# An attention and feed-forward block on one core: layer-norm statistics of odd tiles on ScalarE, key/value groups re-timed on VectorE and GpSimd, division issued in another place, two weight loads moved

## The chip, the cores and the metric

The kernel runs on one core of a Trainium2 chip. The metric is device time in microseconds (us). A core has a matmul engine (TensorE, "PE" in the profile; its weight loads are shown as "PEld"), a vector engine (VectorE, "DVE"), an activation engine (ScalarE, "ACT"), a general engine (GpSimd, "POOL") and an engine that here only issues DMAs (SyncE, "SP"). Each has its own queue of instructions and they wait for each other through semaphores. SBUF is the large on-chip memory; PSUM is the small one, where matmuls accumulate; the program uses it in banks of 512 fp32 columns.

The mean TensorE clock granted in the profiled executions was 0.999 or 1.0. Ratios are compared between calls, microseconds only within one.

## The reference

```python
x = A_x                                                     # 1 x 2048 x 1024, bf16
# attention:
qkv = layernorm(x) @ wqkv                                   # 32 heads of 32
phi = lambda t: jnp.where(t > 0, t + 1, jnp.exp(t)) + 1e-6
pq, pk = phi(q), phi(k)
kv  = einsum("bhsd,bhse->bhde", pk, v);   z = sum over s of pk
o   = einsum(pq, kv) / (einsum(pq, z) + 1e-6)
h   = x + o @ wo
# feed-forward, F = 3584:
hn  = layernorm(h)
g   = hn @ W_gate
h2  = h + ((g * (g > 0)) * (hn @ W_up)) @ W_down
```

It is linear attention: no row of scores is ever formed. `kv` and `z` are summed over all 2048 tokens first; then each query tile is multiplied with them ("num", which carries the denominator in extra columns), divided, transposed and multiplied with `wo`.

## The kernel before

The program runs in stages: start-up, the first token tiles with plain products, then alternating key groups and value groups for pairs of token tiles (k2 to k7, v3 to v7), eight query groups (q00 to q03, then q10 to q13), an output stage (division, transposes, `wo`, second layer norm), and the feed-forward part, which takes about two thirds of the time.

Keys, values, queries and the feed-forward products use a Strassen-Winograd scheme: a 2 x 2 block product is made of seven block products in place of eight. The price is sums of blocks beforehand (VectorE and GpSimd subtract weights from weights, VectorE adds token blocks) and copies of partial sums from bank to bank (ScalarE). One group:

```python
prod(a, X(0, 0), W(0, 0), True, "P1")
ident_act(bank(b), bank(a), ..., name + "fk1")      # ACT: copy P1 into bank b
hook(1)
prod(f, SX(2), TW(2), True, "P7")
ident_act(s7, bank(f), ..., name + "s7")            # ACT: copy P7 to SBUF
hook(2)
prod(b, SX(1), TW(1), False, "P6")                  # needs fk1
ident_act(bank(c), bank(b), ..., name + "fk2")      # ACT
hook(3)
prod(a, X(1, 0), W(1, 0), False, "P2");  e11(a)     # first of four outputs
hook(4)
prod(c, SX(0), TW(0), False, "P5")                  # needs fk2
ident_act(sc, bank(c), ..., name + "sc")            # ACT
s22 = e22(bank(f), ..., sc); s22[0]()
hook(5)
prod(b, X(1, 1), TW(3), False, "P4")
s21 = e21(bank(b), ..., s7); s21[0]()
hook(6)
prod(c, SX(3), W(1, 1), False, "P3")
pend[1] = list(e12(bank(c), B_bank[c]))             # rest of the outputs: done in
pend[2] = list(s22[1:])                             # hooks 1, 2, 3 of the NEXT group
pend[3] = list(s21[1:])
```

`hook(i)` first runs what the previous group left in `pend[i]`, then the side work of this group. All engines take their instructions in the order in which this code issues them, so a hook decides behind what a side job stands in its engine's queue. The outputs of key and query groups go through `phi`: an exponential on ScalarE, then on VectorE a clamp of it (`min 1, + 1e-6`) and `max(t + 1, clamped)`. In value groups the outputs are an add on VectorE ("value add").

The side work in the key/value groups:

```python
def ln1_stats(st):                       # two bn_stats, one bn_aggr, one add on DVE, pow on Pool
    ln1_k[st] = ln_stats(x1[:, i, :], ...)
    run(pool_q, {5: 8, 6: 5, ...}.get(st, 7) if st >= 5 else 0)   # Pool: weight subtractions

def h_k3(p=p):  kvacc(2p-2); kvacc(2p-1); ln1_stats(2 * p + 4)
def h_v1(p=p):  x_sums(p + 1)                                   # four token-block sums, DVE
def h_v2(p=p):  ln1_norm(2 * p + 4); T1d(2 * p + 4)             # normalise, DMA transpose
def h_v5(p=p):  ln1_stats(2 * p + 5)
def h_v7(p=p):  ln1_norm(2 * p + 5); T1d(2 * p + 5)
k_group(p, {3: h_k3});   v_group(p, {1: h_v2, 3: h_v1, 5: h_v5, 7: h_v7})
```

Here `run(pool_q, n)` issues `n` subtractions to GpSimd with no condition but that their inputs are there.

Query groups and output stage:

```python
def a2(st):                              # num matmuls, then add, reciprocal, multiply on DVE
    ...                                  # ("division"), then the DMA transpose T3d of the result
for r in range(2):
    for ct in range(NG // 2):
        if r == 1: hooks[6] = lambda t=ct: a2(t)
        q_group(r, ct, hooks)
flush()
for t in range(NE, NST + LAG + 1):
    a4(t - LAG)                          # wo matmuls, h = ... + x on DVE, LN2 statistics on ACT
    a4_norm(t - LAG - 1)
    a2(t)
    if t in (5, 7, 9, 11, 18, 19):
        load_w_next()                    # 512 KB weight load, same DMA queue as the transposes
    ...
for q in range(NWR):
    load_wraw(q)                         # raw down-weights: first needed in the feed-forward part
```

## Time and profile before

The time was 759.61 us, the median of three runs (759.15 to 759.61). The page's first part gives each engine's busy time; its fourth part gives what the chain of work that ended last consists of.

```profile
PE 737.7 (97%) x3547; PEld 337.2 (45%) x3603; DVE 545.6 (72%) x1083; ACT 291.2 (38%) x500; POOL 82.3 (11%) x148
...
PE 84%; DVE 8%; ACT 2%; issue 2%; SPq 1%; DMA 1%; POOL 0%; DVEq 0%; ACTq 0%; POOLq 0%
```

TensorE bounds the kernel, but "97% busy" does not say how near the end that is. The Trainium skill, Perfetto Trace Analysis, section "Identifying the Most-Contended Engine", warns that matmul busy time is a poor measure of it, because matmuls are pipelined. The trace agrees: a 512-column matmul has a mean record of 379 ns but the next one starts 216 ns later, so a record covers up the first 0.16 us of every gap. I therefore use starts only: for each stage, its length less the sum of its matmuls, each at the spacing it has in an undisturbed stretch (0.2158 us for 512 columns, 0.0585 us for the short ones of the accumulation and of num). Some matmuls have no record (3547 records beside 3603 weight loads); where a distance is longer by just one spacing, the missing matmul is counted in. What remains is lost TensorE time. The Trainium skill, TensorE: Matmul & The Clock Gate, section "Wait — 56ns, not 53.3ns?", gives 215.7 ns for the warm spacing, which agrees with 0.2158 us.

| stage, before | from to (us) | lost TensorE time (us) |
|---|---|---|
| start-up | 1.4 to 39.0 | 3.68 |
| keys and values | 39.0 to 126.25 | 8.71 |
| query groups q00 to q03 | 126.25 to 152.7 | 1.32 |
| query groups q10 to q13 | 152.7 to 180.6 | 1.87 |
| output stage | 180.6 to 245.24 | 3.79 |
| feed-forward | 245.24 to the end | 0.08 |
| sum | 756.8 | 19.45 |

The view by windows gives busy time of each engine in a stretch. These are the key/value groups, the query groups and the output stage.

```profile
core 0: us, PE busy (x) PEld busy (x) DVE busy (x) ACT busy (x) POOL busy (x), PEclk, DMA share, GB/s
52.30:126.20 73.90, 67.95 (x355) 29.99 (x360) 60.05 (x117) 37.95 (x70) 32.69 (x49) 1.00 0.18 41
126.20:180.60 54.40, 52.98 (x274) 23.16 (x273) 44.78 (x93) 33.14 (x62) 0.00 (x0) 1.00 0.35 107
180.60:245.20 64.60, 61.28 (x345) 30.48 (x352) 47.94 (x66) 29.19 (x43) 20.10 (x48) 1.00 0.84 199
```

In the first stretch DVE is busy 60.05 of 73.9 us: no engine is full on the average, but DVE is nearest to it after PE. What PE waited for is shown by the view of waits of PE (columns after the colon: us in total, times, longest):

```profile
PE ps L602 <- ACT ps L607: 3.9, 7, 1.2
PE ps L602 <- DMA RE<-RE: 2.3, 3, 1.2
PE ps L602 <- ACT RX L607: 1.9, 2, 0.9
PE ps L602 <- DVE RE L989: 0.6, 1, 0.6
```

L607 are the copies on ACT (fk1, fk2, s7, sc), "RE<-RE" are the DMA transposes after the division, L989 is the division. So PE waits for ACT, but ACT is only half busy. Why does ACT come late? Its own waits in 52 to 126 us name DVE, and most of all the value add at L900, which must empty a bank before fk1 may write it:

```profile
ACT ps L607 <- DVE RE L900: 13.3, 7, 3.4
```

And why is DVE late? The groups of instructions by shape, in the same window (columns: busy us, mean ns of one, idle before):

```profile
L644 DVE TENSOR_SCALAR RX<-RX 128x512 bf16<-128x512 bf16 x20 | 9.0, 451 | 11.2 <-ACT RX L640 11.2
L647 DVE SCALAR_TENSOR_TENSOR RE<-RX 128x512 bf16<-128x512 f32 x5 | 4.3, 858 | 0.2
L647 DVE SCALAR_TENSOR_TENSOR RE<-ps,RX 128x512 bf16<-128x512 f32 x10 | 6.9, 692 | 0.3
```

L644 is the clamp, 0.29 us when alone and 451 ns on the average here. L647 is the max of phi: with both inputs in SBUF it takes 858 ns on the average, with one input in PSUM 692. The timeline of all engines around one late product, the start of group k5 (columns: start us, length us, engine, line, operation, output<-input, count, idle before and releaser):

```profile
77.88 3.30 POOL L739 TENSOR_TENSOR RH<-RO 128x256 f16<-128x256 bf16 x4
...
78.79 1.11 DVE L647 SCALAR_TENSOR_TENSOR RE<-RX 128x512 bf16<-128x512 f32 x1
...
79.82 0.76 DVE L644 TENSOR_SCALAR RX<-RX 128x512 bf16<-128x512 bf16 x1
...
81.64 0.74 DVE L764 TENSOR_TENSOR RWG<-RAB 128x512 f16<-128x512 bf16 x2
...
83.23 0.68 DVE L900 TENSOR_TENSOR RE<-ps,RX 128x512 bf16<-128x512 f32 x1
...
83.94 0.58 ACT L607 ACTIVATE ps<-ps 128x512 f32<-128x512 f32 x1 [3.41 <-DVE RE L900]
...
84.58 1.04 PE L602 MATMUL ps<-RC,RWG 128*128 128x512 f16 x4 [1.23 <-ACT ps L607]
```

Read it backwards. The product P6 starts at 84.58 after PE stood still for 1.23 us; it waited for fk1 (83.94), which waited 3.41 us for the value add (83.23), which stood behind the token-block sums (from 81.64), behind clamp and phi. Beside these Pool runs four subtractions from 77.88 to 81.2, and the clamp takes 0.76 us in place of 0.29, the phi op 1.11 in place of 0.69. The late phi ops cost PE once more just before: the copy sc, at 79.93, waits 1.21 us for one of them, and the last product of the value group 0.94 us for sc.

In the query groups the chain runs over ACT. The timeline of ACT in group q01, from fk1 to fk2:

```profile
134.66 0.58 ACT L607 ACTIVATE ps<-ps 128x512 f32<-128x512 f32 x1 [2.04 <-PE ps L602]
135.15 0.59 ACT L640 ACTIVATE RX<-ps 128x512 bf16<-128x512 f32 x1
135.63 0.60 ACT L607 ACTIVATE RX<-ps 128x512 f32<-128x512 f32 x1
...
136.63 0.61 ACT L607 ACTIVATE ps<-ps 128x512 f32<-128x512 f32 x1
```

Between fk1 and fk2 stand the exponential of the last group's e12 (135.15), s7 (135.63) and another exponential; ACT is idle for 2.04 us before fk1.

Last, DVE at the start of the feed-forward part waits for the first raw down-weight load (the view names no releaser, but the trace has the load landing at 253.03 us); after that it is in time, and PE loses 0.08 us in the whole part:

```profile
253.10 1.55 DVE L588 TENSOR_TENSOR RW<-RW 128x512 f16<-128x512 bf16 x4 [4.04 <-issue]
254.58 0.68 DVE L1171 TENSOR_TENSOR RAB<-ps,RAB 128x512 bf16<-128x512 f32 x1
```

### The profile page before, as it was taken

The page shows a single profiled execution, that of the slowest core. Times are in us where ns is not written, and L with a number is a line of the kernel's source. Part 1 is how long each engine was busy: PE and PEld are TensorE (multiplying, and loading weights), DVE is VectorE, ACT ScalarE, POOL GpSimd, SP SyncE. Part 2 cuts the span into 40 slices and gives each one's busy share as a digit, 9 for nine tenths or more (in the row PEclk, how much of TensorE's full clock was granted, in tenths as well). Part 3 has the DMA queues.
Part 4 walks back from the last instruction along what each step waited for, and adds up shares of the span by engine and source line. Part 5 has one row for each costly group of instructions (what it writes and reads, how often), then busy time and mean ns, then how long its engine had stood idle before and what let it go on. Part 6 is the DMA issues. An engine that isn't in the chain of part 4 may idle for free.

```text
span 756.8 us, 10080 instructions
## 1 busy us (share of the span) xinstructions
PE 737.7 (97%) x3547; PEld 337.2 (45%) x3603; DVE 545.6 (72%) x1083; ACT 291.2 (38%) x500; POOL 82.3 (11%) x148
## 2 busy tenths in 40 slices
PE   8999889999999999999999999999999999999998
PEld 3444334344544444444444444444444444444443
DVE  7978885889766798878877584847768686663343
ACT  4344545665850545454454100025454544520000
POOL 2746730000360000000000000000000000000000
PEclk9999999999999999999999999999999999999999
DMA  9753112402799786665445799743232231026664
GB/s 301 199 84 85 29 28 100 166 15 55 180 238 240 234 274 200 186 174 169 139 139 178 227 289 284 229 143 111 61 108 85 83 111 56 1 77 185 207 191 134
DMA packets 160225, 113.38 MB, mean 150 GB/s; under 512 B 51504, under 2 KB 141360, under 8 KB 160176
## 3 DMA queue, kind: packets, MB, share of 16 engines
q1 hardware_dynamic: 160176, 112.75, 52.3%
q8 instruction: 28, 0.46, 0.2%
q14 instruction: 21, 0.17, 0.1%
HBM read 85.46 MB, written 15.73 MB: 134 GB/s over the span
## 4 chain that ended last, share of the span: by engine, by line
PE 84%; DVE 8%; ACT 2%; issue 2%; SPq 1%; DMA 1%; POOL 0%; DVEq 0%; ACTq 0%; POOLq 0%
PE ps L602 84%; ACT ps L607 1%; DVE RX L644 1%; DVE RAB L647 1%; SPq L512 1%; DVE RE L647 1%; DVE RE L989 1%; DVE RWG L764 1%; ACT RX L640 1%; DVE RE L900 1%; DMA RE<-RE 1%; DVE st L615 1%; DVE RX L839 0%; SPq L508 0%; DVE RXH L629 0%
## 5 line engine op out<-in xcount | busy, mean ns | idle before, releaser
L607 ACT ACTIVATE ps<-ps 128x512 f32<-128x512 f32 x150 | 87.5, 583 | 199.5 <-PE ps L602 170.8
L602 PE MATMUL ps<-RC,RO 128*128 128x512 f16 x672 | 154.2, 379 | 0.0
L602 PE MATMUL ps<-RW,RAB 128*128 128x512 f16 (+1 forms) x681 | 150.1, 379 | 0.6
L602 PEld LDWEIGHTS ps<-RW,RAB 128*128 128x128 bf16 (+1 forms) x692 | 67.7, 98 | 81.6
L602 PE MATMUL ps<-RH,RWG 128*128 128x512 bf16 x435 | 103.0, 379 | 0.7
L602 PEld LDWEIGHTS ps<-RC,RO 128*128 128x128 f16 x672 | 65.7, 98 | 79.3
L607 ACT ACTIVATE RE<-ps 128x512 f32<-128x512 f32 x120 | 71.0, 597 | 76.1 <-PE ps L602 53.9
L602 PE MATMUL ps<-RC,RWG 128*128 128x512 f16 x296 | 71.1, 379 | 2.8 <-ACT ps L607 2.8
L602 PEld LDWEIGHTS ps<-RH,RWG 128*128 128x128 bf16 x448 | 43.8, 98 | 52.9
L1171 DVE TENSOR_TENSOR RAB<-ps,RAB 128x512 bf16<-128x512 f32 x28 | 19.3, 690 | 65.4 <-PE ps L602 65.4
L602 PE MATMUL ps<-RW,RE 128*128 128x512 bf16 x248 | 57.0, 379 | 2.8 <-DMA RE<-RE 2.3
L602 PE MATMUL ps<-RH,RO 128*128 128x512 bf16 (+1 forms) x242 | 58.3, 379 | 0.7
L602 PE MATMUL ps<-RAB 128*128 128x512 bf16 x239 | 56.6, 379 | 1.3 <-ACT RAB L691 0.7
L607 ACT ACTIVATE RAB<-ps 128x512 bf16<-128x512 f32 x56 | 33.4, 597 | 61.6 <-PE ps L602 61.6
L1102 DVE TENSOR_TENSOR RO<-RWG,RO 128x512 f16<-128x512 bf16 x108 | 45.3, 420 | 1.8
L602 PEld LDWEIGHTS ps<-RC,RWG 128*128 128x128 bf16 (+1 forms) x296 | 28.5, 98 | 38.9 <-ACT ps L607 5.4
L623 POOL TENSOR_TENSOR rstd<-ve,neghalf 128x1 f32<-128x1 f32 x24 | 14.4, 601 | 281.2 <-DVE ve L620 281.2
L1178 DVE TENSOR_TENSOR RE<-ps,RE 128x512 f32<-128x512 f32 x56 | 38.4, 690 | 5.0 <-ACT RE L607 5.0
L1102 DVE TENSOR_TENSOR RO<-RWG 128x512 f16<-128x512 bf16 x108 | 40.6, 417 | 0.0
L615 DVE BATCH_NORM_STATS2 st<-RE 128x6 f32<-128x512 bf16 x48 | 30.7, 680 | 12.8 <-DMA RE<-h_scr 11.9
L644 DVE TENSOR_SCALAR RX<-RX 128x512 bf16<-128x512 bf16 x64 | 23.1, 361 | 22.3 <-ACT RX L640 22.3
L1183 DVE TENSOR_TENSOR RE<-ps,RE 128x512 f32<-128x512 f32 x56 | 38.1, 681 | 0.0
(114 smaller groups left out, 792.0 us busy)
## 6 DMA issues: line engine op xcount, KB each, us to landing
RWG<-in_B_W_gate_dram SPq DMA_DIRECT2D x28, 512.0 KB, 3.7
RWG<-in_B_W_up_dram SPq DMA_DIRECT2D x28, 512.0 KB, 4.7
RW<-t_scr SPq DMA_DIRECT2D x56, 256.0 KB, 3.2
RW<-in_B_W_down_dram SPq DMA_DIRECT2D x42, 256.0 KB, 3.8
RW<-in_B_W_down_dram SPq DMA_DIRECT2D x14, 512.0 KB, 4.0
t_scr<-RW SPq DMA_DIRECT2D x14, 512.0 KB, 4.9
RE<-in_A_x_dram SPq DMA_DIRECT2D x23, 256.0 KB, 4.7
RAB<-in_A_wqkv_dram SPq DMA_DIRECT2D x8, 512.0 KB, 8.2
```

The costliest lines, as they stand in the source:

```text
L512: return PL.add("sp", lambda e: e.dma_start_transpose(dst_ap, src_ap), reads=reads, writes=writes, slot=slot, name=name)
L602: lambda e: e.matmul(out_ap, lhsT, rhs, start=start, stop=stop, skip_group_check=skip),
L607: PL.add("act", lambda e: e.activation(out=dst, in_=src, func=func), reads=reads, writes=writes, name=name)
L615: PL.add("dve", lambda e, c=c: e.bn_stats(out=st6[:, k, c * 6:(c + 1) * 6], in_=src_full[:, c * BCH:(c + 1) * BCH]), reads=[src_chunk_bufs ...
L623: PL.add("pool", lambda e: e.tensor_tensor(out=rstd[:, k, :], in0=ve[:, k, :], in1=neghalf[:], op=ALU.pow), reads=[B_ve[k], B_neghalf], wr ...
L640: PL.add("act", lambda e: e.activation(out=Et[:, k, :], in_=src, func=ACTF.Exp), reads=[src_buf], writes=[B_E[k]], name=name + "_exp")
L644: PL.add("dve", lambda e: e.tensor_scalar(out=Et[:, k, :], in0=Et[:, k, :], scalar1=1.0, scalar2=1e-6, op0=ALU.min, op1=ALU.add), reads=[] ...
L647: PL.add("dve", lambda e: e.scalar_tensor_tensor(out=dst_ap, in0=src, scalar=C1, in1=Et[:, k, :], op0=ALU.add, op1=ALU.max), reads=[src_bu ...
L1102: PL.add(eng, lambda e: e.tensor_tensor(out=Tring[:, k, j], in0=in0, in1=in1, op=ALU.subtract), reads=reads, writes=[B_T[k][j]], name="T%d ...
L1171: PL.add("dve", lambda e: e.tensor_tensor(out=hh[:, f1, 0:SBW], in0=bank(BA[1]), in1=r11[:, rr, :], op=ALU.mult), reads=[B_bank[BA[1]], B_ ...
L1178: PL.add("dve", lambda e, w=w: e.tensor_tensor(out=ftmp[:, 4 + w, :], in0=bank(BF_[w]), in1=ftmp[:, 2 + w, :], op=ALU.add), reads=[B_bank[ ...
L1183: PL.add("dve", lambda e, w=w: e.tensor_tensor(out=ftmp[:, 6 + w, :], in0=bank(BB[w]), in1=ftmp[:, w, :], op=ALU.add), reads=[B_bank[BB[w] ...
```

## The change

The intent: take work off DVE where it makes ACT and PE late, keep Pool away from DVE's sensitive ops, and let transposes leave earlier. The diff, cut to its core (renamed buffers and unchanged arithmetic left out):

```diff
+        def act_stats(src, src_bufs, junk, junk_buf, sv, svb, name):
+            def mean():   # ACT: Identity, scale 1/D, accum_out
+            def square(): # ACT: Square, scale D**-0.5, accum_out; then three small ops on Pool
+            return mean, square
+        def pool_piece(n=1):
+            for _ in range(min(n, len(pool_q))):
+                pool_q.pop(0)(PL.prog["act"][-1])   # waits for the ACT op issued last
         def ln1_stats(st):
-            run(pool_q, {5: 8, 6: 5, 7: 4, 8: 5, 9: 5, 10: 5}.get(st, 7) if st >= 5 else 0)
         # w_sums:
-                def go(d):
+                def go(d, dep):
                     PL.add(eng, ... op=ALU.subtract), reads=reads, writes=[btw[j]],
+                           deps=[dep], name=...)
         # sgroup, after P3:
-            pend[1] = list(e12(bank(c), B_bank[c]))
+            s12 = list(e12(bank(c), B_bank[c]))
+            if isq:                       # query groups only
+                s12.pop(0)()              # the exponential of e12, at once
+            pend[1] = s12
         # key/value groups, A, B = 2p + 4, 2p + 5:
+            def h_k1(): pool_piece(2); ln1_stats(A)      # last two p: x_sums instead
             def h_k3(): kvacc(2p-2); kvacc(2p-1)
-                        ln1_stats(2 * p + 4)
-            def h_v1(): x_sums(p + 1)
-            def h_v2(): ln1_norm(2 * p + 4); T1d(2 * p + 4)
-            def h_v5(): ln1_stats(2 * p + 5)
-            def h_v7(): ln1_norm(2 * p + 5); T1d(2 * p + 5)
-            k_group(p, {3: h_k3}); v_group(p, {1: h_v2, 3: h_v1, 5: h_v5, 7: h_v7})
+            def h_k5(): pool_piece(2); m_, q_ = ln1_stats_act(B); m_(); sq.append(q_)
+            def h_k6(): q_(); x_sums(p + 1)
+            def h_v3(): pool_piece(2)                    # last two p only
+            def h_v5(): pool_piece(2)
+            def h_v6(): ln1_norm and T1d of A, then of B
+            k_group(p, {1: h_k1, 3: h_k3, 5: h_k5, 6: h_k6})
+            v_group(p, {3: h_v3, 5: h_v5, 6: h_v6})
         # query groups:
-                    hooks[6] = lambda t=ct: a2(t)
+                    hooks[6] = lambda t=ct: a2_num(t)
                 q_group(r, ct, hooks)
+                if r == 1:
+                    pend[1].insert(1 if ct + 1 < NG // 2 else 0, lambda t=ct: a2_div(t))
         # output stage:
-                a4(t - LAG)
+                a4_mm(t - LAG)
+                a2_num(t); a2_div(t)
+                a4_h(t - LAG)
                 a4_norm(t - LAG - 1)
-                a2(t)
-            if t in (5, 7, 9, 11, 18, 19):
+            if t in (5, 7, 18, 19):
                 load_w_next()
+        load_w_next()
+        load_w_next()
         for q in range(NWR):
             load_wraw(q)
```

So the division of query tile t no longer stands in hook 6 of its own group but in hook 1 of the next, behind the clamp of the phi whose exponential was issued early; and in the output stage it stands in front of h, not behind it.

## The prediction

> **What bounds the kernel.** TensorE: page part 1 gives PE 97% of a 756.8 us span, and part 4 puts 84% of the last chain on matmul. In the timeline the feed-forward part (245 us to the end, about two thirds of the span) starts a 512-column matmul every 0.216 us without a gap; nothing is to be won there. Pricing every matmul at that rate (the 128-column ones at 0.059) leaves 19.4 us of lost PE time, an estimate from those starts, all before 245 us: start-up 3.7, key/value groups (52 to 126 us) 8.8, query groups (126 to 181) 3.2, output stage (181 to 245) 3.8. The change leaves the start-up alone, so 15.7 us (2.1%) is the most it can win.
>
> **Key/value groups.** By windows, DVE is 90% busy in 66 to 98 us, PE 87%. The timeline shows why: beside Pool's subtractions (0.67 us each) the bf16 clamp takes 0.75 us instead of 0.29, the phi op 1.11 instead of 0.69, the normalisation 0.91 instead of 0.54. The Trainium skill, SBUF — State Buffer, "Who interferes with whom", says that such DVE ops contend with GpSimd for a shared port pair; these durations agree. DVE then runs late, ACT's evictions wait for it ("ACT waited for DVE", 11.3 us in 54 to 110 us), and PE waits 1.5 to 1.8 us before each late product. The change takes about 1.7 us of DVE statistics per pair of tiles away, gates Pool's pieces behind chosen ACT ops, and moves the token-block sums out of the crowded place. It adds two ACT passes per odd tile, about 2.3 us (1.06 each plus the accumulator reads, as in the output stage), put where ACT idles 2.04 us before the value group's first eviction; so they delay that one by 0.1 to 0.3 us. I expect this stage to keep 2.5 to 3.3 us of its loss: gain 5.8.
>
> **Query groups.** The exponential issued before the next group's first eviction takes one 0.5 us step from the ACT chain that ends in the second "fk2" copy, where PE waits (0.25 to 0.45 us per group). In the last four DVE is nearly full (7.0 us of work in 7.0), and the first num matmul after them waits 1.0 us for the division behind h. Issuing exponentials early and h after the division gains 0.9 + 2.0.
>
> **Output stage.** PE waits 2.9 us for transposes that land late (a backlog in the DMA queue: the transpose of tile 12 is ready at 219.7, issued at 226.4). Earlier division, and weight loads 2 and 3 out of the way, should remove nearly all: gain 2.8.
>
> **Given back.** Loads 2 and 3 now stand in front of loads 4, 5 and the first raw down-weight load, which already holds DVE for 4.0 us at 249 to 253 us. I expect that load about 3 us later, DVE late in the first feed-forward pair, and PE losing about 1 us there: a new gap where there was none.
>
> **Sum.** 5.8 + 2.9 + 2.8 - 1.0 = 10.5, less 0.7 for surprises: 749.8 us, 8 in 10 between 747.2 and 753.2. Faster by over 2%: 0.03; within 2%: 0.96; slower: 0.01.
>
> **What would show it.** Right: DVE clamp and phi ops mostly at 0.29 and 0.69 us; no PE gap over 1 us before 126 us; no PE wait on the RE transposes; feed-forward starting about 11 us earlier; a DVE wait on the raw weight load longer than 4.0 us. Wrong: value-group evictions waiting for the ACT statistics by over 0.5 us; DVE waiting for the paired xn transposes (2.7 us to land before); Pool still stretching DVE; a stall of 2 us or more in the first two feed-forward pairs.

## The result and the profile after

The changed kernel took 749.0 us (median of four runs, 748.72 to 749.52) beside 759.53 (759.15 to 759.61). The ratio is 0.9863, 95% interval 0.9846 to 0.988. It is computed as the mean time of the fast runs of one kernel over that of the other's of the same rounds, so it is not quite the ratio of the medians. By the measure used here (2%) the two are the same; the predicted 749.8 us is close, and the range 747.2 to 753.2 held. A repeat on another chip gave 749.3 us and 0.987.

Parts 1 and 4 of the page:

```profile
PE 737.0 (99%) x3547; PEld 337.8 (45%) x3603; DVE 537.3 (72%) x1067; ACT 299.9 (40%) x516; POOL 87.5 (12%) x148
...
PE 89%; DVE 4%; ACT 3%; issue 2%; SPq 0%; DMA 0%; DVEq 0%; POOL 0%; ACTq 0%; POOLq 0%
```

The span of the profiled execution went from 756.8 to 747.4 us. PE has the same 3547 matmuls and the same busy time, in a shorter span; DVE's share of the last chain fell from 8 to 4%. The windows of the same three stages, with the same columns as before:

```profile
52.80:120.40 67.60, 66.74 (x355) 30.01 (x360) 51.56 (x105) 44.24 (x82) 31.64 (x48) 1.00 0.22 48
120.40:173.20 52.80, 52.80 (x274) 23.09 (x272) 42.50 (x89) 34.19 (x62) 0.00 (x0) 1.00 0.38 110
173.20:234.60 61.40, 60.64 (x346) 30.63 (x352) 48.24 (x66) 29.18 (x43) 19.55 (x40) 1.00 0.82 193
```

The key/value stretch is 6.3 us shorter for the same 355 matmuls; DVE does 8.5 us less in it and ACT 6.3 us more. The query stretch is 1.6 and the output stage 3.2 us shorter. PE's waits in the whole span are now these; the 1.4 us behind Pool are in the start-up and were there before:

```profile
PE ps L604 <- POOL RXH L475: 1.4, 1, 1.4
...
PE ps L604 <- DVE RE L1219: 0.6, 1, 0.6
PE ps L604 <- DVE RXH L1062: 0.4, 1, 0.4
PE ps L604 <- ACT ps L609: 0.2, 1, 0.2
```

The waits behind ACT's copies fell from 5.8 us (3.9 and 1.9) to 0.2, and those behind the transposes are gone. Two are new: L1219, in the feed-forward part, and L1062, the op that computes h in the output stage. ACT no longer waits for a value add in 52 to 126 us; its longest waits are for PE itself:

```profile
ACT ps L609 <- PE ps L604: 16.0, 14, 2.1
```

The groups of DVE in the same window: the clamp's mean went from 451 to 294 ns, that of the phi op with both inputs in SBUF from 858 to 752. The timeline of DVE from 77 to 81 us shows single ops: the clamp takes 0.29, phi 0.69 and the normalisation 0.54 us (0.84 on the average before). The first fence is the groups, the second the timeline.

```profile
L667 DVE TENSOR_SCALAR RX<-RX 128x512 bf16<-128x512 bf16 x22 | 6.5, 294 | 18.3 <-ACT RX L663 18.2
L670 DVE SCALAR_TENSOR_TENSOR RE<-RX 128x512 bf16<-128x512 f32 x7 | 5.3, 752 | 0.2
```

```profile
77.00 0.29 DVE L667 TENSOR_SCALAR RX<-RX 128x512 bf16<-128x512 bf16 x1
77.33 0.69 DVE L670 SCALAR_TENSOR_TENSOR RE<-RX 128x512 bf16<-128x512 f32 x1
...
80.47 0.54 DVE L652 TENSOR_SCALAR RXH<-RE,mv,rstd 128x1024 bf16<-128x1024 bf16 x1
```

ACT in query group q01, from fk1 to fk2: the exponential between fk1 and s7 is gone. But the distance of fk1 to fk2 shrank only from 1.97 us (136.63 less 134.66) to 1.83 (130.70 less 128.87), since s7 now waits 0.23 us for PE to finish P7.

```profile
128.87 0.58 ACT L609 ACTIVATE ps<-ps 128x512 f32<-128x512 f32 x1 [0.32 <-PE ps L604]
129.68 0.60 ACT L609 ACTIVATE RX<-ps 128x512 f32<-128x512 f32 x1 [0.23 <-PE ps L604]
...
130.70 0.59 ACT L609 ACTIVATE ps<-ps 128x512 f32<-128x512 f32 x1
```

And DVE at the start of the feed-forward part, which is now at 234.7 us: two new waits for the moved weight loads, then the raw down-weight load, which lands 10.84 us after that start in place of 7.8. DVE's later results come late for it: PE's wait for L1219 above lies there, at 249.4 us.

```profile
237.10 0.76 DVE L1143 TENSOR_TENSOR RO<-RWG 128x512 f16<-128x512 bf16 x2 [0.72 <-DMA RWG<-in_B_W_gate_dram]
...
240.76 0.76 DVE L1143 TENSOR_TENSOR RO<-RWG 128x512 f16<-128x512 bf16 x2 [2.10 <-DMA RWG<-in_B_W_up_dram]
...
245.61 1.55 DVE L590 TENSOR_TENSOR RW<-RW 128x512 f16<-128x512 bf16 x4 [4.09 <-issue]
```

Lost TensorE time by stage, in the profiled executions of both kernels and of all experiments, computed as before. The rows are used in the next section.

| kernel | start | keys, values | q00 to q03 | q10 to q13 | output | feed-forward | sum |
|---|---|---|---|---|---|---|---|
| before | 3.68 | 8.71 | 1.32 | 1.87 | 3.79 | 0.08 | 19.45 |
| after | 4.19 | 2.41 | 1.06 | 0.60 | 0.56 | 1.23 | 10.05 |
| e1_loads_back | 4.32 | 2.42 | 1.06 | 0.60 | 0.63 | 0.08 | 9.11 |
| e2_before_loads_late | 4.49 | 8.75 | 1.33 | 1.86 | 0.79 | 1.14 | 18.36 |
| e3_loads_16_17 | 3.63 | 2.42 | 1.06 | 0.60 | 0.56 | 0.08 | 8.35 |
| e4_stats_on_dve | 4.59 | 2.66 | 1.06 | 0.72 | 0.60 | 1.62 | 11.25 |
| e5_pool_ungated | 4.31 | 3.88 | 1.06 | 0.60 | 0.56 | 0.83 | 11.24 |
| e6_before_pool_gated | 4.03 | 8.92 | 1.33 | 1.87 | 3.95 | 0.08 | 20.18 |
| e7_h_before_division | 3.68 | 2.43 | 1.05 | 0.60 | 1.57 | 1.06 | 10.39 |
| e8_q_exp_late | 3.85 | 2.43 | 1.33 | 4.66 | 0.62 | 1.51 | 14.40 |
| e9_after_again | 3.74 | 2.43 | 1.06 | 0.60 | 0.56 | 1.40 | 9.79 |
| e10_loads_16_17_k_exp | 4.15 | 2.12 | 1.05 | 0.60 | 0.56 | 0.08 | 8.56 |
| e11_placing_only | 3.68 | 5.03 | 1.06 | 0.72 | 0.59 | 1.22 | 12.30 |
| e12_before_gated_sums_qexp | 4.03 | 3.63 | 1.06 | 1.58 | 3.98 | 0.08 | 14.36 |

Two things help in reading it. A stage between the start and the feed-forward part that an edit does not touch repeats mostly to some 0.02 us, at worst to 0.2 (the output stage of the kernels built on the one before), although each line is another program. So the stages hardly act on each other, and one look tells more than a timed ratio whose interval is 2 us wide. The first column is the exception: it moves between 3.63 and 4.59 with no edit in its place. At the start the matmuls run cold, 0.427 us apart, and between seven and twelve of the first ones ran so before the clock rose, 4.5 to 7.4 us into the span. The Trainium skill, TensorE: Matmul & The Clock Gate, section "What's actually happening", lets the array's recent activity decide when the throttle goes; the number of cold matmuls agrees with the clock's rise not being tied to an instruction. But that is not all of the spread: e3 and e4 both have nine cold matmuls and lost 3.63 and 4.59 us. In e4 PE waited 1.0 us for a load of `wqkv`, in e3 it did not. So up to about 1 us of a difference between two profiled spans can come from the start-up alone. The feed-forward column also moves by some tenths where the loads stand at the end (0.83 to 1.62): it depends on when a transfer lands.

### The profile page after: what moved, and what is told of

Read it like the earlier page. It is cut to its first block, busy times and chain, and to the rows that moved or that the text cites. A ratio compares the mean times of both kernels' runs of the same rounds, so it can differ in the third digit from the quotient of the medians.

```text
span 747.4 us, 10100 instructions
## 1 busy us (share of the span) xinstructions
PE 737.0 (99%) x3547; PEld 337.8 (45%) x3603; DVE 537.3 (72%) x1067; ACT 299.9 (40%) x516; POOL 87.5 (12%) x148
## 4 chain that ended last, share of the span: by engine, by line
PE 89%; DVE 4%; ACT 3%; issue 2%; SPq 0%; DMA 0%; DVEq 0%; POOL 0%; ACTq 0%; POOLq 0%
PE ps L604 89%; DVE RAB L670 1%; ACT ps L609 1%; ACT RX L663 1%; ACT RX L609 1%; DVE RX L667 1%; DVE RE L1038 1%; ACT RXH L633 0%; ACT RXH L638 0%; DVE RX L884 0%; SPq L510 0%; DVE RXH L1062 0%; DMA RW<-in_B_W_down_dram 0%; DVE rden L1036 0%; PE ps L728 0%
## 5 line engine op out<-in xcount | busy, mean ns | idle before, releaser
L625 POOL TENSOR_TENSOR rstd<-rstd,neghalf 128x1 f32<-128x1 f32 x20 | 12.6, 632 | 251.5 <-DVE rstd L622 251.5
L1219 DVE TENSOR_TENSOR RE<-ps,RE 128x512 f32<-128x512 f32 x56 | 38.3, 691 | 5.0 <-ACT RE L609 4.8
L604 PEld LDWEIGHTS ps<-RH,RO 128*128 128x128 f16 (+1 forms) x256 | 24.6, 98 | 29.8 <-ACT RX L609 1.5
L667 DVE TENSOR_SCALAR RX<-RX 128x512 bf16<-128x512 bf16 x64 | 19.9, 311 | 24.0 <-ACT RX L663 23.9
```

Of the source, the lines that this page charges most:

```text
L604: lambda e: e.matmul(out_ap, lhsT, rhs, start=start, stop=stop, skip_group_check=skip),
L625: PL.add("pool", lambda e: e.tensor_tensor(out=rstd[:, k, :], in0=rstd[:, k, :], in1=neghalf[:], op=ALU.pow), reads=[B_neghalf], writes=[B ...
L667: PL.add("dve", lambda e: e.tensor_scalar(out=Et[:, k, :], in0=Et[:, k, :], scalar1=1.0, scalar2=1e-6, op0=ALU.min, op1=ALU.add), reads=[] ...
L1219: PL.add("dve", lambda e, w=w: e.tensor_tensor(out=ftmp[:, 4 + w, :], in0=bank(BF_[w]), in1=ftmp[:, 2 + w, :], op=ALU.add), reads=[B_bank[ ...
```

## The experiments

The theory to be tested was the prediction's: the key/value gain comes from less DVE work and from keeping Pool off DVE's ops; the query gain from the early exponential and the division's new place; the output gain from transposes that leave earlier; and the two late loads cost about 1 us. The rivals: one part alone does it all and the others are idle or harmful; or the placing of side jobs in the queues does it, not the contention.

### e1: the two loads back in their old places

```diff
-            if t in (5, 7, 18, 19):
+            if t in (5, 7, 9, 11, 18, 19):
                 load_w_next()
-        load_w_next()
-        load_w_next()
```

> The changed kernel with gate/up weight loads 2 and 3 issued inside the output stage again, where they were before. Theory (the two parts of the output-stage change are separable: earlier division alone gives the transposes enough lead, the late loads only cost): the output stage still loses less than 1.0 us of PE time, with no PE wait on the RE transposes over 0.3 us, the 1.2 us gap in the first feed-forward pairs is gone, and the median is about 748.0 us. Rival (the moved loads are what freed the transposes): PE waits for RE transposes come back with 1 us or more in total, and the median is 749.5 to 751 us although the feed-forward gap is gone.

Measured: 748.39 us beside 758.69 (0.986, 0.9846 to 0.9873). The gap in the feed-forward part is gone (1.23 to 0.08 us) and PE waits for no transpose (output stage 0.63). With the loads in their old places the transpose of tile 12 was ready at 211.6, was issued at 215.6 and landed at 220.4 us, still in time. So the early division alone mends the transposes, and the late loads were not needed for it; they cost 1.15 us. The timed ratio cannot show that 1 us (after: 0.9863), the stage does.

### e2: the kernel before, with only the two loads moved

```diff
-            if t in (5, 7, 9, 11, 18, 19):
+            if t in (5, 7, 18, 19):
                 load_w_next()
...
+        load_w_next()
+        load_w_next()
```

> The kernel before with only loads 2 and 3 moved behind the output stage. Theory: the transposes' backlog shrinks by roughly 3 us, so PE's 2.3 us of waits for RE transposes fall below 0.7 us, but the raw down-weight load lands about 3 us later and PE loses about 1.2 us in the first feed-forward pairs: net gain 1 us, about 758.5 us. Rival (only the order of division and h matters for the transposes): the waits stay at about 2 us, the feed-forward loss is added, and the median is 760 to 761 us.

Measured: 756.9 us beside 758.69 (0.9975, 0.9962 to 0.9987). The output stage falls from 3.79 to 0.79 us, the feed-forward part rises from 0.08 to 1.14. So moving the loads alone also mends the transposes, at a net gain of about 1.9 us by stage and 1.8 by the clock, nearly twice the 1 us that was forecast. Either half of the change suffices; the changed kernel does both and pays for the second.

### e3: the two loads between the old and the new place

```diff
-            if t in (5, 7, 18, 19):
+            if t in (5, 7, 16, 17, 18, 19):
                 load_w_next()
-        load_w_next()
-        load_w_next()
```

> The changed kernel with loads 2 and 3 issued in steps 16 and 17 of the output stage, right after the last RE transpose, so they can delay none. Theory: no wait comes back in the output stage, the raw down-weight load lands within 5.5 us of the feed-forward start as it did before, the 1.2 us gap is gone: about 747.8 us, 1.1 us under the changed kernel. Rival (the feed-forward gap has another cause than the queue in front of the raw load, for example the four weight-difference ops on VectorE): the gap stays and the median is 748.7 to 749.3 us.

Measured: 748.27 us beside 758.69 (0.9858, 0.9845 to 0.9872). Output 0.56, feed-forward 0.08: no cost on either side. The raw load lands about 8.3 us after the start of the feed-forward part, near the 7.8 of the kernel before, though later than the 5.5 that was expected. The sum of losses, 8.35, is the lowest of all kernels here, though 0.56 of its lead over the changed kernel is start-up, which is not the edit's.

### e4: statistics of odd tiles on DVE again, everything else as changed

```diff
             def h_k1(...):
                     ln1_stats(A)
+                    ln1_stats(B)
             def h_k5(...):
                 pool_piece(2)
-                if B < NST: m_, q_ = ln1_stats_act(B); m_(); sq.append(q_)
```

> The changed kernel with the statistics of odd tiles back on VectorE, put behind those of the even tile early in the key group, where VectorE idles 2.3 us per group; no statistics on ScalarE. Theory (Pool's contention and the placing made VectorE late, not the amount of work): key/value groups keep the same loss within 0.4 us, perhaps 0.2 us less since the value group's first eviction no longer waits for the ScalarE passes; 748.6 to 749.4 us. Rival (taking 1.7 us of VectorE work per pair away is what cured it): evictions wait for VectorE again, the key/value groups lose 1.5 us or more extra, and the median is 750.5 us or more.

Measured: 750.17 us beside 758.69 (0.9883, 0.9867 to 0.9898). The key/value stage lost only 2.66 in place of 2.41 us, most of it in v3 (0.84 us in place of 0.43). The rest of the difference to the changed kernel lies in the start (+0.4) and the feed-forward part (+0.4), which the edit does not touch. So the part of the change that its title names first is worth about 0.25 us once the others are in: the expectation for the stage held, the timed one missed for reasons outside it.

### e5: Pool's pieces not gated, everything else as changed

```diff
-                           reads=reads, writes=[btw[j]], deps=[dep], name=...)
+                           reads=reads, writes=[btw[j]], name=...)
```

> The changed kernel with Pool's weight-difference pieces in the same program order but not held behind a ScalarE op any more (their data waits stay). Theory (contention on the shared ports is what made VectorE late, and the gating removes it): VectorE's clamp and phi ops stretch again in many of the key/value groups (0.75 and 1.11 us instead of 0.29 and 0.69), value-group evictions wait for VectorE, and the median rises by 1 to 3 us, to 750 to 752 us. Rival (the gating is decoration, the relief came from less work on VectorE): the median stays within 0.5 us of 749.0 us and the key/value groups lose no more than 0.5 us extra.

Measured: 750.15 us beside 758.94 (0.9883, 0.9869 to 0.9896). The stage lost 3.88 us (+1.5), nearly all in v4, 1.54 us in place of 0.43, and v5, 0.70. The clamp, in the groups by shape:

```profile
L667 DVE TENSOR_SCALAR RX<-RX 128x512 bf16<-128x512 bf16 x21 | 8.4, 402 | 9.7 <-ACT RX L663 9.7
```

402 ns on the average: ungated pieces fall on clamp and phi again. Gating is worth 1.5 us with the new placing.

### e6: the kernel before, with only the gating

Pool's pieces get the changed kernel's gate and schedule, DVE's and ACT's instructions keep the old order.

```diff
-            run(pool_q, {5: 8, 6: 5, 7: 4, 8: 5, 9: 5, 10: 5}.get(st, 7) if st >= 5 else 0)
+    # deps=[dep] in w_sums; pool_piece(6), (4), (2) ... as in the changed kernel
-            k_group(p, {3: h_k3})
+            k_group(p, {1: h_pool, 3: h_k3, 5: h_pool})
-            v_group(p, {1: h_v2, 3: h_v1, 5: h_v5, 7: h_v7})
+            v_group(p, {1: h_v2, 3: h_v3, 5: h_v5p, 7: h_v7})   # h_v3: h_v1 + pool in the last two
```

> The kernel before with only Pool's pieces cut into the changed kernel's schedule and held behind the same ScalarE ops; statistics, token-block sums and normalisations stay where they were on VectorE. Theory (contention): VectorE's ops mostly return to 0.29 and 0.69 us, and the key/value groups' 8.8 us loss falls to 3 to 6 us: 754 to 757 us. Rival (work and placing): the loss stays above 7.5 us and the median within 1.3 us of 759.5 us.

Measured: 759.65 us beside 758.94 (1.0008, 0.9996 to 1.0021). The clamp came down to 307 ns, as forecast, and the stage lost 8.92 us, as much as before. The forecast from contention failed: the ops it named were mended and nothing was won. The timeline of this run at the place shown of the kernel before tells why:

```profile
80.44 0.69 DVE L647 SCALAR_TENSOR_TENSOR RE<-RXH,RX 128x512 bf16<-128x512 f32 x1
81.05 1.23 DVE L767 TENSOR_TENSOR RWG<-RAB 128x512 f16<-128x512 bf16 x2
...
81.18 1.63 POOL L742 TENSOR_TENSOR RH<-RO 128x256 f16<-128x256 bf16 x2 [4.98 <-ACT RX L607]
...
82.31 0.78 DVE L767 TENSOR_TENSOR RWG<-RWG,RAB 128x512 f16<-128x512 f16 x1
...
83.47 0.68 DVE L903 TENSOR_TENSOR RE<-ps,RX 128x512 bf16<-128x512 f32 x1
...
84.18 0.58 ACT L607 ACTIVATE ps<-ps 128x512 f32<-128x512 f32 x1 [3.15 <-DVE RE L903]
```

Phi is done by 81.1 us in place of 81.7, but the gated pieces of Pool (81.18) now fall on the token-block sums (L767): the first two take 1.23 us where they took 0.74 before, the third 0.78 where it took 0.42. The value add behind them starts at 83.47 (83.23 before), and ACT's wait for it is 3.15 us. The contention moved to the next op of the same queue. Over 52 to 126 us, ACT's waits for the value add grew from 13.3 to 15.7 us:

```profile
ACT ps L607 <- DVE RE L903: 15.7, 8, 3.7
```

### e7: h in front of the division again

```diff
                 a4_mm(t - LAG)
+                a4_h(t - LAG); a4_norm(t - LAG - 1)
                 a2_num(t); a2_div(t)
-                a4_h(t - LAG); a4_norm(t - LAG - 1)
```

> The changed kernel with the residual add and the normalisation of the output stage issued before the num matmuls and the division of the same step, as before; loads 2 and 3 stay late. Theory: each transpose is issued about 1.2 us later, and the first num matmul waits about 1 us for the division behind h again, but the backlog without the two loads is short, so the transposes themselves are not waited for: loss of 0.5 to 1.2 us, 749.5 to 750.2 us. Rival (the order is what gave the transposes their lead): PE waits on RE transposes come back with 1 us or more and the median is 750.7 us or more.

Measured: 749.99 us beside 758.94 (0.9882, 0.9867 to 0.9897). The output stage lost 1.57 in place of 0.56 us: PE waits 0.9 us once for a division that stands behind h, and 0.4 us once for a transpose. The rest of the output stage's gain stays, since the moved loads still hold. The expectation held.

### e8: exponentials of the query groups late again

The division then has to go behind that phi's clamp and max (place 2 of the list in place of 1).

```diff
             s12 = list(e12(bank(c), B_bank[c]))
-            if isq:
-                s12.pop(0)()
...
-                    pend[1].insert(1 if ct + 1 < NG // 2 else 0, lambda t=ct: a2_div(t))
+                    pend[1].insert(2 if ct + 1 < NG // 2 else 0, lambda t=ct: a2_div(t))
```

> The changed kernel with the query groups' exponential put back behind the next group's first eviction. Theory: ScalarE's chain to the second copy of a query group is one op (0.5 us) longer, PE waits 0.68 us or more between products in place of 0.52 to 0.57, the seven query groups after the first lose 0.15 to 0.3 us each: 1.1 to 2 us in all, 750.2 to 751 us. Rival (VectorE's 6.7 us per late group bounds them, the exponential's place does not matter there): only the three early groups lose, 0.3 to 0.6 us in all, 749.3 to 749.7 us.

Measured: 753.85 us beside 758.94 (0.9932, 0.992 to 0.9945). Both forecasts were far too low: the query stage lost 5.99 us in place of 1.66, more than the 3.19 of the kernel before. In q00 to q03, which have no division, the loss is the old one (1.33). In q11, q12, q13 it is 1.55, 1.38 and 1.39. The timeline of DVE shows the step that I had not thought of:

```profile
155.86 0.29 DVE L667 TENSOR_SCALAR RX<-RX 128x512 bf16<-128x512 bf16 x1 [1.65 <-ACT RX L663]
...
157.40 1.22 DVE L1036 TENSOR_TENSOR RE<-ps,rden 128x1024 bf16<-128x1024 f32 x1
```

DVE stands idle for 1.65 us, waiting for the late exponential, and the division that was ready all the time stands behind that wait, because the queue keeps its order. The rest of the group's phi work then comes late. So the two edits of the query groups belong together: the early exponential's worth by itself is 0.26 us in four groups, but it is what makes the division's new place affordable.

### e9: the changed kernel again

No edit; a repeat beside the next three on the same chip.

> The changed kernel itself, on the same chip and in the same rounds as the next one, as its yardstick: ratio to the kernel before 0.986 to 0.987, losses by stage as in its first profile (key/value 2.4 us, query 1.7, output 0.6, first feed-forward pairs 1.2).

Measured: 749.3 us beside 759.04 (0.987, 0.9857 to 0.9884). All stages but the start (3.74) and the feed-forward part (1.40) repeat to 0.02 us.

### e10: a version meant to beat both

e3, and the early exponential in the last two key groups too.

```diff
-                   add_phi(*dst(1, 1), "k_%d_1" % (2 * p + 1)), "k%d" % p, hooks)
+                   add_phi(*dst(1, 1), "k_%d_1" % (2 * p + 1)), "k%d" % p, hooks, p >= NST // 2 - 2)
...
-            if t in (5, 7, 18, 19):
+            if t in (5, 7, 16, 17, 18, 19):
                 load_w_next()
-        load_w_next()
-        load_w_next()
```

> The changed kernel with loads 2 and 3 in steps 16 and 17, and with the last two key groups (which have no statistics on ScalarE behind them) issuing their late exponential before the value group's first eviction, as the query groups do. By the stage losses: 1.15 us less in the first feed-forward pairs and 0.25 us less in each of the last two value groups, 1.6 us under the changed kernel of the same call. Rival (what is taken away in one place is waited for in the next): under 0.8 us of difference.

Measured: 747.96 us (747.78 to 748.05) beside e9's 749.3 (748.79 to 749.42) and 759.04 of before; 0.9854 (0.984 to 0.9867). It beats both kernels, the changed one by 1.3 us; no run of either touches the other's. Groups v6 and v7 lost 0.19 in place of 0.35 us each, and the feed-forward gap is gone. By stages the gain over e9 is 1.64 us; the start took back 0.4.

### e11: the new placing alone

e4 and e5 together: no statistics on ACT, no gate.

```diff
-                           reads=reads, writes=[btw[j]], deps=[dep], name=...)
+                           reads=reads, writes=[btw[j]], name=...)
...
                     ln1_stats(A)
+                    ln1_stats(B)
...
-                if B < NST: m_, q_ = ln1_stats_act(B); m_(); sq.append(q_)
```

> The changed kernel with both the statistics back on VectorE and Pool's pieces not held behind ScalarE ops, so that in the key/value groups only the new places of sums, statistics and normalisations remain. If the three parts add up, the key/value loss is about 2.4 + 0.25 + 1.5 = 4.1 us; if the fuller VectorE makes the contention count for more, 4.7 to 6.5 us. Rival to the importance of placing: 8 us or more, as before the change.

Measured: 751.9 us beside 759.04 (0.9907, 0.9893 to 0.992). The key/value stage lost 5.03 us. With the new placing the four combinations are thus:

| lost in keys and values (us) | statistics on ACT | statistics on DVE |
|---|---|---|
| Pool gated | 2.41 | 2.66 |
| Pool not gated | 3.88 | 5.03 |

Adding the two single losses to 2.41 gives 4.13; measured was 5.03, so the two parts partly stand in for each other. And the placing alone takes the stage from 8.71 to 5.03: 3.7 of the 6.3 us.

### e12: the kernel before, gated, with the sums moved and the exponentials early

e6, with `x_sums` in hook 6 of the key group in place of hook 3 of the value group, and `isq` for the query groups; the division stays in hook 6.

```diff
-            k_group(p, {1: h_pool, 3: h_k3, 5: h_pool})
+            k_group(p, {1: h_pool, 3: h_k3, 5: h_pool, 6: h_k6})     # h_k6: x_sums(p + 1)
...
+            if isq:
+                s12.pop(0)()
```

> The kernel before with Pool's pieces held back as in the earlier run, plus one thing in each of two stages that do not touch each other. Key/value groups: the token-block sums moved from the value group to the end of the key group. If their old place in front of the value adds is what kept ScalarE waiting, the stage's loss falls from 8.9 us to 4 us or less; if the rest of the placing is needed, it stays above 6.5 us. Query groups: the exponential issued early, the division left where it was. If the early exponential is enough, all query groups lose as little as in the changed kernel (late ones 0.2 us each); if the division has to move as well, only the early groups gain (0.1 to 0.16 us each) and the late ones stay at 0.4 us or more, since the phi op that frees the bank then sits behind the division.

Measured: 752.7 us beside 759.04 (0.9918, 0.9904 to 0.9932). The key/value stage lost 3.63 us, where e6 lost 8.92. ACT's waits for a value add (now L906), 15.7 us in e6, are down to this:

```profile
ACT ps L607 <- DVE RE L906: 0.2, 1, 0.2
```

Every later key group loses 0.11 us and every later value group 0.35, and what is left is v3 (1.80). One edit on top of the gate, which moves four sums from in front of the value adds, wins 5.3 of the 6.3 us. In the query groups the first four gained what the changed kernel gains (1.06), while q11 to q13 kept 0.49 each: there the division must move as well.

## Why the prediction was right

The predicted time, 749.8, was 0.8 us above the measured 749.0. Point by point:

- **Key/value groups, predicted gain 5.8:** measured 6.30 (8.71 less 2.41). The loss kept, 2.41, is just under the predicted 2.5 to 3.3. The two ACT passes put off the value group's first copy by about 0.08 us, where 0.1 to 0.3 was said. The effect of Pool on DVE that the prediction named is there: the clamp's mean is 294 ns after and 451 before, and the Trainium skill, SBUF — State Buffer, section "Who interferes with whom", agrees with the traces in which ops suffer. But the weight that the prediction gave to it was only half right. The gate by itself won nothing (e6), the placing by itself 3.7 us (e11), and gate and moved sums together, on the old kernel, 5.1 (e12); the moved sums without the gate and without the rest of the placing were not run. The prediction named "moves the token-block sums out of the crowded place" in half a sentence; that was the key. The statistics on ACT, named first, are worth 0.25 us with the gate, and 1.15 without (5.03 less 3.88).
- **Query groups, predicted 0.9 + 2.0:** this is the mis-sized term. The first four groups gained 0.26 us and the last four 1.27; with the wait of the first num matmul after them (0.74 to 0 us), and a new wait of 0.55 us of the third `wo` product for h, about 1.7 us in all, where 2.9 was said. (These two waits are counted in the output stage of the table. They are taken from matmul starts, as the table is; the prediction's 1.0 here, and its 2.9 for the transposes, are idle times of weight loads.) The step that failed was that a half-microsecond op taken out of ACT's chain shortens it by as much. s7 moved up until it met the end of P7 and then waited 0.23 us for PE, so the chain shrank by 0.14 us only (1.97 to 1.83).
- **Output stage, predicted 2.8:** the waits for late transposes fell by 3.0 us, from 3.0 to 0.01, by matmul starts. The transpose of tile 12 was ready at 219.66, issued at 226.42 and landed at 230.93 us before; after, 211.44, 213.79 and 216.89, with 4.1 us to spare. e1 and e2 show that either half of what the prediction named suffices.
- **Given back, predicted 1.0:** 1.15 us. The raw load lands 3.06 us later, measured from the start of the feed-forward part, where about 3 was said. e1 and e3 show that the loads cause it: with them elsewhere the loss is 0.08. One detail was not foreseen: DVE's wait on the raw load itself hardly grew (4.04 to 4.09 us); DVE waits 0.72 and 2.10 us for the moved loads first.
- **Sum:** 6.30 + 1.7 + 3.0 - 1.15 = 9.85 us; the profiled span fell by 9.4, with 0.5 us more lost in the start-up, and the timed medians fell by 10.5. The query term was 1.2 us too high; the 0.7 us held back for surprises and a key/value term that was 0.5 too low made up for it. That the total was better than its parts is luck.
- **Signs named beforehand:** between 40 and 126 us the longest distance of two matmul starts is 0.49 us (no gap over 1 us, as said; the start-up, which the change leaves alone, keeps its idle times of 1.37 us before the first matmul and 0.73 us at 11 us); the feed-forward part starts 10.55 us earlier (about 11 was said). One sign for "wrong" appeared in part: Pool still stretches some DVE ops, now mostly the token-block sums (the first two of a group take 517 ns on the average, 415 before), but no wait of ACT names them any more. The others did not appear.

What stays open: why ungated Pool pieces cost most in v4, why e12 still loses 1.80 us in v3, and when the first loads land in the start-up.

## What to carry to other kernels

On an in-order engine, ask for each side job which urgent op stands behind it in the queue. Keeping two engines from contending helps only if the freed time is not taken by the next op of the same queue: here the gate alone won 0 us, and with four sums moved out of the way 5.1. Where two repairs aim at the same wait, try each alone: early division or late loads would each have mended the transposes, and doing both cost 1.15 us, which loads placed in between did not.

## What the Trainium skill lacked or had wrong

- SBUF — State Buffer, "Who interferes with whom": it does not name the phi op (scalar_tensor_tensor) or bn_stats; they fall under its rules by the number of inputs in SBUF, and the runs agree. Here scalar_tensor_tensor with both inputs in SBUF went from 0.69 to 1.11 us beside Pool's subtractions, with one input in PSUM it stayed at 0.69, and a bn_stats of 512 columns took 0.68 us with and without Pool.
- ScalarE: Activation LUTs: the page has no cost for reading the accumulator after an activation (`accum_out`). Here that is a separate 0.19 us, and it is 1.18 us from one such activation of 1024 elements (1.06 us) to the next.
- DMA: Bandwidth & Descriptors: its only times for an SBUF-to-SBUF transpose are cycle counts for one of 8,192 tiles. No time was found there for how long one of 128 x 1024 bf16 holds the queue that issues it, or for its way to landing. In the kernel before, a transpose held the queue for 1.23 us in most cases and up to 2.49, a plain DMA mostly for 0.3 to 0.6 us; from issue to landing a transpose took 2.7 to 5.8 us.
